# Attention scores as a stream of full banks, a ring of three probability buffers, and a last row tile in column parts

## The chip, the cores and the metric

One Trainium2 chip; the program runs on one of its cores. The metric is the device time of one execution in microseconds (us). TensorE (PE) multiplies matrices and writes its results to PSUM, which the kernel uses as eight banks of 512 fp32 values per partition. ScalarE (ACT), VectorE (DVE) and GpSimd (POOL) work element by element; ACT and DVE read PSUM here. SyncE (SP) issues most of the transfers of the DMA engines, in its program's order; POOL and ACT issue some.

## The reference

Causal attention with 16 "beacon" keys that every query may see, and then a two-layer network with a squared ReLU on the attention's output.

```python
B, H, S, Nb, D = (8, 8, 576, 16, 64)
k_all = np.concatenate([beacon_k, k], axis=2)          # 592 keys per head
v_all = np.concatenate([beacon_v, v], axis=2)
scores = scale * np.matmul(q, k_all.transpose(0, 1, 3, 2))
causal = np.zeros((S, Nb + S), dtype=bool)
causal[:, Nb:] = np.triu(np.ones((S, S), dtype=bool), k=1)
scores = np.where(causal, -1000000000.0, scores)
a = np.exp(scores - scores.max(-1, keepdims=True))
a /= a.sum(-1, keepdims=True) + 1e-09
attn_out = np.matmul(a, v_all)                          # [8, 8, 576, 64]
x = attn_out.transpose(0, 2, 1, 3).reshape(B * S, H * D)  # 4608 tokens x 512
r = np.maximum(x @ w_in, 0.0)                           # w_in 512 x 2048
out = (r * r) @ w_out                                   # w_out 2048 x 512
```

The kernel computes in bf16 with fp32 sums. It leaves the maximum out of the exponential and divides by the sum at the end.

## The kernel before, in words

**Tiling.** Keys and queries are cut into five tiles (`NT`) of 128 positions; the last has 80. The kernel works on pairs of heads: 8 batches of 4 pairs, 32 pairs. Scores are computed transposed, keys on the partitions and queries along the row, so that the exponentials can be the stationary operand of the next matmul. Only what the causal mask leaves is computed: key tile `c` meets the queries from its own start to 576. That makes 1664 columns a pair for each head.

**Scores** (L589). The two heads of a pair sit on partitions 0 to 63 and 64 to 127, and a matmul for each head uses half of PE's rows. They write to a *strip*, two PSUM banks, one per head. There are two strips. In batches 1 to 7 a pair has four pieces of 496, 464, 416 and 288 columns (`WHOLE`), and PE visits the scores twice a pair: two pieces fill both strips, and four more matmuls per head the next two. That is eight visits a batch. Batch 0 has its own cut (`SPLIT`), in two phases, one piece a visit.

**Exponentials** (L604): ACT reads both heads of a piece at once and writes bf16 probabilities to a buffer `pt`; there are four, one for each pair in flight. **Mask** (L614, L618): DVE takes the smaller of the probabilities and 0 or a large number on the diagonal blocks. Four blocks go in one instruction, and the last block of 80 in a second one. **Values** (L639): 15 matmuls for each head with the probabilities as weights and 65 columns of `vb`, v with a column of ones that gives the sum. **Normalise** (L657, L659): DVE divides, into `xn`. Then `xn` is transposed into `xT`: on PE for batches 0 to 2 (L707), by DMA transposes that SP issues for later ones (L690).

**The network.** Chunks of 512 tokens. First layer (L770): 16 tiles of four matmuls, each in a bank, evicted with ReLU by ACT (L786) or DVE (L788), squared by DVE (L795). Second layer (L805): for each of four row tiles of 128 tokens 16 matmuls into one bank, a copy to `osb` (L297 on ACT, L299 on DVE), and a store for every two row tiles (L833), in the last chunk for each (L831).

**PSUM** is full: two strips (four banks) and a pool `ps` of four banks for everything else: first layer, second layer, values, transposes.

**Loads.** q, k and v come in fp32 into eight staging buffers `stg` (L344), are cast by POOL (L299), and for batches 2 to 7 q and k are transposed into `qT` and `kT` by two DMA transposes a batch (L376). SP's queue holds these loads, these transposes, those of `xn` and the stores, in one order. POOL issues the loads of batches 0 and 1 and of the weights.

**The order** is worked out when the program is built. Every piece of work is an `Op` with a duration, a priority, what it needs and which buffers it takes from pools; `Order.run` (L67 on) walks through time, gives each engine the ready piece of least priority value, and so fixes each engine's instruction order. Score pieces also have a gate (L559): they may not start before a certain amount of network work has been placed. On the chip only the order is left, with semaphores for the needs.

## Time and profile before

| | |
|---|---|
| runs | 345.93, 347.67, 347.45 us; median 347.45 |
| the profiled execution: span, first to last instruction | 345.0 us (its own time is given only as this span) |
| PE busy | 327.1 us, 95% |
| ACT busy | 194.7 us, 56% |
| DVE busy | 168.4 us, 49% |
| POOL busy | 90.7 us, 26% |
| score matmuls, L589 | 400, 36.0 us |
| exponentials, L604 | 128, 103.6 us |
| masks, L614 and L618 | 36 and 32; 23.6 and 11.5 us |
| values matmuls, L639 | 960, 40.3 us |
| first and second layer, L770 and L805 | 133.2 and 131.2 us |
| granted PE clock | 1.00 |

Busy time of PE counts each matmul from its start to a modelled end, and matmuls overlap, so a busy PE says that there was no gap and not how fast it was; differences between starts say that. Some matmul records are missing (551 of 576 are there for L805), so a group of three may have been four. In the timeline a line is: start, length, engine, line, operation, tiles, shape, count, and in brackets the idle time before it with what ended it. In the table by stretch a line is: stretch, length, then busy time and count of PE, weight loads, DVE, ACT and POOL, granted clock, DMA share, GB/s.

### The profile page before, as it was taken

The numbers are of one execution on the slowest core, as the hardware profiler recorded it, in microseconds if no ns is written. First come the engines' busy times: TensorE is split into PE (matmuls) and PEld (weight loads), VectorE is DVE, ScalarE is ACT, GpSimd is POOL, SyncE is SP. The second block draws the span as 40 slices with busy tenths as digits, with TensorE's granted clock in tenths as the row PEclk, the third lists the DMA queues.
The fourth block names the chain that finished last, engine by engine and source line by source line (L and its number), as shares of the span: only waits on it lengthen the run. The fifth ranks groups of instructions, "written<-read, shape, count | busy, mean of one in ns | idle before, by whom it ended". The sixth has DMA issues, their size and how long they took to land.

```text
span 345.0 us, 7128 instructions
## 1 busy us (share of the span) xinstructions
PE 327.1 (95%) x2829; PEld 174.0 (50%) x2868; DVE 168.4 (49%) x372; ACT 194.7 (56%) x297; POOL 90.7 (26%) x141
## 2 busy tenths in 40 slices
PE   2799899999998999999999999999999999999995
PEld 1567675544553444444456855544554444444442
DVE  5888884158534873575355546457533302401400
ACT  4796674377645764576656655577536416515611
POOL 9844703316414504250153115312000000000000
PEclk9999999999999999999999999999999999999999
DMA  9999969999999999998699979984014011011002
GB/s 169 220 206 220 205 101 209 214 240 211 177 219 198 232 182 170 209 221 176 142 256 207 178 148 208 228 204 101 2 64 128 0 61 63 0 61 64 0 21 101
DMA packets 145291, 51.88 MB, mean 150 GB/s; under 512 B 132458, under 2 KB 140010, under 8 KB 145258
## 3 DMA queue, kind: packets, MB, share of 16 engines
q1 hardware_dynamic: 135741, 42.45, 61.4%
q0 software_dynamic: 8512, 8.49, 14.5%
q10 hardware_dynamic: 1005, 0.49, 0.6%
q8 instruction: 22, 0.36, 0.5%
q14 instruction: 11, 0.09, 0.1%
HBM read 37.22 MB, written 9.44 MB: 135 GB/s over the span
## 4 chain that ended last, share of the span: by engine, by line
PE 78%; DMA 11%; SPq 3%; ACT 3%; POOL 2%; issue 1%; DVE 1%; DVEq 0%; ACTq 0%; POOLq 0%
PE ps L805 32%; PE ps L770 31%; PE ps L639 7%; DMA stg<-in_v_dram 6%; PE strip L589 6%; ACT pt L604 2%; DMA stg<-in_k_dram 2%; DMA stg<-in_q_dram 1%; DMA osb<-in_k_dram 1%; SPq L344 1%; SPq L376 1%; POOL vb L299 1%; POOL qk_area L299 1%; PE ps L451 1%; PE ps L707 0%
## 5 line engine op out<-in xcount | busy, mean ns | idle before, releaser
L770 PE MATMUL ps<-xT,w_in 128*128 128x512 bf16 (+3 forms) x690 | 133.2, 340 | 0.6
L805 PE MATMUL ps<-w_out,g 128*128 128x512 bf16 x551 | 131.2, 379 | 1.9 <-issue 0.8
L604 ACT ACTIVATE pt<-strip 128x832 bf16<-128x832 f32 (+4 forms) x128 | 103.6, 867 | 38.4 <-PE strip L589 38.2
L786 ACT ACTIVATE g<-ps 128x512 bf16<-128x512 f32 (+2 forms) x128 | 72.0, 562 | 47.9 <-PE ps L770 47.4
L770 PEld LDWEIGHTS <-w_in 128*128 128x128 bf16 x704 | 65.2, 98 | 57.6 <-issue 6.5
L795 DVE TENSOR_TENSOR g<-g 128x1024 bf16<-128x1024 bf16 (+2 forms) x80 | 52.4, 659 | 76.5 <-ACT g L786 75.3
L805 PEld LDWEIGHTS <-g 128*128 128x128 bf16 x576 | 52.5, 98 | 60.0 <-issue 3.2
L299 POOL CAST qk_area<-stg 128x512 bf16<-128x512 f32 (+2 forms) x60 | 39.3, 662 | 53.2 <-DMA stg<-in_k_dram 31.8
L299 POOL CAST vb<-stg 128x512 bf16<-128x512 f32 (+1 forms) x38 | 26.2, 697 | 87.4 <-DMA stg<-in_v_dram 83.0
L297 ACT COPY osb<-ps 128x512 f32<-128x512 f32 x26 | 15.2, 586 | 50.8 <-PE ps L805 44.5
L639 PEld LDWEIGHTS <-pt 128*128 128x128 bf16 (+1 forms) x960 | 36.4, 98 | 14.7 <-issue 3.4
L639 PE MATMUL ps<-vb,pt 128*128 128x65 bf16 (+1 forms) x960 | 40.3, 194 | 3.0 <-POOL vb L299 2.9
L589 PE MATMUL strip<-qT,kT 64*128 64x80 bf16 (+7 forms) x400 | 36.0, 283 | 2.2 <-ACT pt L604 1.0
L659 DVE TENSOR_TENSOR xn<-ps,rcp 128x320 bf16<-128x320 f32 (+2 forms) x64 | 31.5, 492 | 2.4 <-DVE rcp L657 0.2
L614 DVE TENSOR_TENSOR pt<-pt,tri 128x1024 bf16<-128x1024 bf16 (+1 forms) x36 | 23.6, 656 | 13.4 <-ACT pt L604 13.4
L657 DVE RECIPROCAL rcp<-ps 128x5 f32<-128x5 f32 (+2 forms) x64 | 12.3, 192 | 34.6 <-PE ps L639 34.4
L788 DVE TENSOR_SCALAR g<-ps 128x512 bf16<-128x512 f32 (+2 forms) x32 | 19.1, 599 | 9.9 <-PE ps L770 9.2
L589 PEld LDWEIGHTS <-kT 64*128 64x128 bf16 x400 | 12.8, 95 | 21.6 <-issue 17.0
L299 DVE COPY osb<-ps 128x512 f32<-128x512 f32 x10 | 6.9, 692 | 14.9 <-PE ps L805 14.6
L618 DVE TENSOR_TENSOR pt<-pt,tri 80x160 bf16<-80x160 bf16 x32 | 11.5, 359 | 0.0
L344 POOL DMA_DIRECT2D stg<-in_v_dram x10 | 8.5, 854 | 6.9 <-DMA w_in<-in_moe_w_in_dram 5.5
L451 PE MATMUL ps<-ident,qk_area 120*128 120x120 bf16 x16 | 2.5, 299 | 6.5 <-DVE qk_area L299 6.4
(39 smaller groups left out, 68.6 us busy)
## 6 DMA issues: line engine op xcount, KB each, us to landing
out_dram<-osb SPq DMA_DIRECT2D x17, 512.0 KB, 3.7
stg<-in_q_dram SPq DMA_DIRECT2D x24, 256.0 KB, 4.9
stg<-in_k_dram SPq DMA_DIRECT2D x18, 256.0 KB, 5.2
stg<-in_v_dram SPq DMA_DIRECT2D x18, 256.0 KB, 4.7
w_in<-in_moe_w_in_dram POOLq DMA_DIRECT2D x4, 512.0 KB, 11.1
w_out<-in_moe_w_out_dram POOLq DMA_DIRECT2D x4, 512.0 KB, 11.6
stg<-in_v_dram POOLq DMA_DIRECT2D x6, 256.0 KB, 8.4
stg<-in_k_dram SPq DMA_DIRECT2D x6, 224.0 KB, 4.2
```

The lines of the kernel that those rows point to most:

```text
L297: nc.scalar.copy(dst, src)
L299: eng[e].tensor_copy(dst, src)
L589: nc.tensor.matmul(st[:, hj, at:at + t1 - t0], kT[b % 2][hp, pr, 128 * c:128 * c + 128], qT[b % 2][hp, pr, t0:t1], start=True, stop=True,)
L604: nc.scalar.activation(pt[take_pt.held[2]][:, :, off:off + width], st[:, :, 0:width], AF.Exp, bias=0.0, scale=scale)
L614: nc.vector.tensor_tensor(out=d, in0=d, in1=tri[:, m0:m0 + m, :][:, None].to_broadcast([128, 2, m, 128]), op=ALU.min)
L639: nc.tensor.matmul(a[:, at + (t - tl[0]) * (D + 1):at + (t - tl[0] + 1) * (D + 1)], P[0:rr, hj, o:o + 128], vb[b % 2][0:rr, c, 2 * pr + hj ...
L659: nc.vector.tensor_tensor(out=xn[b % 2].rearrange("p t (h d) -> p h t d", d=D)[:, h0:h0 + nh, tl[0]:tl[0] + nt], in0=a[:, :, :, 0:D], in1= ...
L770: nc.tensor.matmul(h[:, lo - spans[0][0]:hi - spans[0][0]], w_in_sb[:, mc, ft * 128:(ft + 1) * 128], xT[:, mc, lo % RING:lo % RING + hi - lo],
L786: nc.scalar.activation(dst, h, AF.Relu, bias=0.0, scale=1.0)
L788: nc.vector.tensor_scalar(out=dst, in0=h, scalar1=0.0, scalar2=None, op0=ALU.max)
L795: nc.vector.tensor_tensor(out=d, in0=d, in1=d, op=ALU.mult)
L805: nc.tensor.matmul(o, G[:, fc, ts * 128:(ts + 1) * 128], w_out_sb[:, fc, :], start=(fc == 0), stop=(fc == NFT - 1))
```

## The change

Three things.

*Scores of batches 1 to 7.* The four pairs of a batch are laid end to end: 4 x 1664 columns are 13 pieces of exactly 512, so that each head's half of a piece fills one bank. The segments of a pair are ordered anew (`SEGS`), and a piece may end one pair and begin the next. A batch has five visits of 2, 3, 3, 3, 2 pieces (2, 2, 3, 3, 3 in batches 1 and 2, `PLAN`). The first two pieces of a visit go to the strips. The third takes two banks of the pool `ps`, one for each head, and its exponentials are one instruction for each head. A piece that wraps around the ring of probabilities has its exponential in two parts.

*Probabilities.* One buffer that holds three pairs of 1664 columns in a ring, instead of four buffers of 2048; batch 0 has a spare slot for its fourth pair. The gaps that had to be cleared are gone, and so are eight memsets. Masks are three instructions a pair (two blocks, two blocks, the last 80), each of which waits only for the exponentials of its own columns. Batch 0's pieces are cut to the same 1664 columns: 368, then 416, 416 and 464. The gate of a visit is computed from where its first column lies. An `Op` may now take from several pools.

*The last row tile.* The last 128 tokens' second layer is done in column parts of 256, 128 and 128, each with its own 16 matmuls, its own copy (DVE, ACT, DVE) and its own store (SP, SP, ACT).

The planner's durations for scores, masks and values are changed a little too, and so the order of everything else shifts.

```diff
-        self.take = (*take, 1)[:3] if take else None
-        self.give = give
+        self.take = [(*t, 1)[:3] for t in (take if isinstance(take, list) else [take])] if take else []
+        self.give = give if isinstance(give, list) else [give] if give is not None else []
...
-    NSTG, NPT, RB = 8, 4, 4
+    NSTG, NPT, RB = 8, 3, 4
+    PW = 1664
...
-    pt = [sb(f"pt{i}", [128, 2, 2048], BF16) for i in range(NPT)]
+    pt = sb("pt", [128, 2, NPT * PW], BF16)
+    pt_spare = sb("pt_spare", [128, 2, PW], BF16)
...
-    for p in pt:
-        nc.vector.memset(p[:, :, 928:1952].rearrange("p h (a w) -> p h a w", w=512)[:, :, :, 0:96], 0.0)
-        nc.vector.memset(p[:, :, 1824:2048], 0.0)
...
+    SEGS = [(0, 0, 240), (0, 368, 576), (1, 112, 576), (2, 240, 576), (3, 368, 576), (4, 496, 576), (0, 240, 368)]
+    seg_at, whole_off = [0], {}
+    for c, t0, t1 in SEGS:
+        for t in range(c, NT):
+            if t0 <= t_start(t) and t_start(t) + t_rows(t) <= t1:
+                whole_off[c, t] = seg_at[-1] + t_start(t) - t0
+        seg_at.append(seg_at[-1] + t1 - t0)
+    assert seg_at[-1] == PW and len(whole_off) == NT * (NT + 1) // 2
...
-        pieces=[
-            ([(0, 0, 496, 0)], 0, 496),
-            ([(1, 112, 576, 0)], 512, 464),
-            ([(2, 240, 576, 0), (0, 496, 576, 336)], 1024, 416),
-            ([(3, 368, 576, 0), (4, 496, 576, 208)], 1536, 288),
-        ],
-        diag=(0, 512, 0, 4), last=1744, tiles=range(NT), off=whole_off)]
+        pieces=None,
+        diag=[(0, 448, 0, 2), (912, 336, 2, 2), (1456, 0, 1, 1)],
+        tiles=range(NT), off=whole_off)]
...
-                ([(2, 240, 576, 0), (4, 496, 576, 336)], 512, 416),
-                ([(3, 368, 576, 0), (0, 240, 496, 208)], 1024, 464),
-                ([(1, 240, 576, 0), (0, 496, 576, 336)], 1536, 416),
+                ([(2, 240, 576, 0), (4, 496, 576, 336)], 368, 416),
+                ([(3, 368, 576, 0), (0, 496, 576, 208), (1, 240, 368, 288)], 784, 416),
+                ([(1, 368, 576, 0), (0, 240, 496, 208)], 1200, 464),
...
+    def slot_of(p):
+        return (p - HP) % NPT if p >= HP else p
+
+    def prob(p):
+        if p < HP and slot_of(p) == NPT:
+            return pt_spare
+        return pt[:, :, slot_of(p) * PW:(slot_of(p) + 1) * PW]
+
+    def freed(p):
+        if p < HP:
+            return []
+        return av_ops[p - NPT] if p >= HP + NPT else av_ops[p - HP]
...
+    PLAN = {1: (2, 2, 3, 3, 3), 2: (2, 2, 3, 3, 3)}
+
+    def add_stream(b):
+        for pr in range(HP):
+            p = HP * b + pr
+            qk_ops[p], av_ops[p], exps_of[p] = [], [], []
+        done, k = 0, 0
+        for n in PLAN.get(b, (2, 3, 3, 3, 2)):
+            visit, pairs, cols = [], [], 0
+            for k in range(k, k + n):
+                mms, outs = [], []
+                lo, hi = 512 * k, 512 * k + 512
+                for pr in range(HP):
+                    for i, (c, t0, t1) in enumerate(SEGS):
+                        a = pr * PW + seg_at[i]
+                        z = a + t1 - t0
+                        if a < hi and z > lo:
+                            x, y = max(a, lo), min(z, hi)
+                            mms.append((pr, c, t0 + x - a, t0 + y - a, x - lo))
+                            cols += max(64, y - x)
+                    x, y = max(pr * PW, lo), min((pr + 1) * PW, hi)
+                    if x < y:
+                        if pr not in pairs:
+                            pairs.append(pr)
+                        outs.append((pr, x, y))
+                visit.append((mms, outs, lo))
+            k += 1
+            first = HP * b + pairs[0]
+            base = 100.0 * first
+            box = {}
+
+            def banks(box, s):
+                qk = box["qk"]
+                if s < 2:
+                    st = strips[qk.slots["strip"][s]]
+                    return st[:, 0], st[:, 1]
+                return tuple(ps[i] for i in qk.slots["ps"])
+
+            def emit_qk(e, visit=visit, box=box):
+                for s, (mms, _, _) in enumerate(visit):
+                    for pr, *mm in mms:
+                        score_mm(b, pr, banks(box, s), *mm)
+
+            deps = []
+            for pr in pairs:
+                deps += qk_deps(b, pr, 0) + freed(HP * b + pr)
+            at = HP * b + visit[0][2] / PW
+            qk = add(f"qk{first}.{k}", "PE", 0.21 + cols / 2400.0, emit_qk, prio=base + k, deps=deps,
+                     take=[("strip", "strip", 2)] + ([("ps", "sc", 2)] if n > 2 else []), gate=gate_at(at))
+            box["qk"] = qk
+            for pr in pairs:
+                qk_ops[HP * b + pr].append(qk)
+            for s, (mms, outs, lo) in enumerate(visit):
+                runs = []
+                for pr, x, y in outs:
+                    p = HP * b + pr
+                    a = slot_of(p) * PW + x - pr * PW
+                    if runs and runs[-1][0] + runs[-1][1] - runs[-1][2] == a:
+                        runs[-1][1] = y
+                        runs[-1][3].append((p, x - pr * PW, y - pr * PW))
+                    else:
+                        runs.append([a, y, x, [(p, x - pr * PW, y - pr * PW)]])
+                for hjs in ([(0, 1)] if s < 2 else [(0,), (1,)]):
+                    prev = []
+                    for i, (a, y, x, whose) in enumerate(runs):
+                        def emit_exp(e, a=a, x=x, y=y, lo=lo, hjs=hjs, box=box, s=s):
+                            if len(hjs) == 2:
+                                out, in_ = pt[:, :, a:a + y - x], strips[box["qk"].slots["strip"][s]][:, :, x - lo:y - lo]
+                            else:
+                                out, in_ = pt[:, hjs[0], a:a + y - x], banks(box, s)[hjs[0]][:, x - lo:y - lo]
+                            nc.scalar.activation(out, in_, AF.Exp, bias=0.0, scale=scale)
+
+                        give = None
+                        if i == len(runs) - 1:
+                            give = (qk, s, "strip") if s < 2 else (qk, hjs[0], "ps")
+                        ex = add(f"exp{first}.{k}.{s}.{hjs[0]}.{i}", "ACT", 0.18 + len(hjs) * (y - x) / 1200.0, emit_exp,
+                                 prio=(base + k + 0.1 * s + 0.01 * hjs[0]) * 1.0e-4 - (30.0 if b > 1 else 12.0), deps=[qk], behind=prev, give=give)
+                        prev = [ex]
+                        for p, r0, r1 in whose:
+                            exps_of[p].append((ex, r0, r1))
+            while done < HP and (done + 1) * PW <= 512 * k:
+                add_phase(b, done, HP * b + done, 0, WHOLE[0])
+                done += 1
...
+        masks = []
+        for i, (at, step, m0, m) in enumerate(ph.diag):
+            rows, w = (128, 128) if step else (LAST, LAST)
+
+            def emit_mask(e, at=at, step=step, m0=m0, m=m, rows=rows, w=w):
+                d = prob(p)[0:rows, :, at:at + max(w, m * step)].rearrange("p h (c w) -> p h c w", c=m)[:, :, :, 0:w]
+                nc.vector.tensor_tensor(out=d, in0=d, in1=tri[0:rows, m0:m0 + m, 0:w][:, None].to_broadcast([rows, 2, m, w]),
+                                        op=ALU.min)
+
+            lo, hi = at, at + (m - 1) * step + w
+            masks.append(add(f"mask{p}.{n}.{i}", "DVE", 0.12 + 2 * m * w / 1920.0, emit_mask, prio=base + 0.1 * i,
+                             deps=[ex for ex, x, y in exps_of[p] if x < hi and y > lo] + [tri_op]))
...
+                     deps=masks + [ex for ex, _, _ in exps_of[p]] + [cast[b, "v", c] for c in range(tl[-1] + 1)]
+                     + av_ops[p][-1:], take=("ps", "av"))
...
+    def add_last(j, ts, base, G, sq):
+        u = 2 * j + ts // 2
+        t0 = j * TCH + ts * 128
+        for n, (c0, c1) in enumerate([(0, 256), (256, 384), (384, 512)]):
+            prev, first = None, {}
+            for hf in range(2):
+                def emit_s2(e, hf=hf, first=first, c0=c0, c1=c1):
+                    o = ps[first["s2"].held[2]]
+                    for fc in range(8 * hf, 8 * hf + 8):
+                        nc.tensor.matmul(o[:, 0:c1 - c0], G[:, fc, ts * 128:(ts + 1) * 128],
+                                         w_out_sb[:, fc, c0:c1], start=(fc == 0), stop=(fc == NFT - 1))
+
+                prev = add(f"s2.{j}.{ts}.{n}.{hf}", "PE", 8 * (c1 - c0 + 6) / 2400.0, emit_s2,
+                           prio=base + 130 + 2 * n + hf, deps=sum(sq[4 * hf:4 * hf + 4], []) + [prev],
+                           take=None if hf else ("ps", "mlp"), pe_time=8 * (c1 - c0 + 6) / 2400.0)
+                first.setdefault("s2", prev)
+
+            def emit_ev(e, first=first, c0=c0, c1=c1):
+                copy_on(e, osb[u % 2][:, ts % 2, c0:c1], ps[first["s2"].held[2]][:, 0:c1 - c0])
+
+            ev = add(f"ev{j}.{ts}.{n}", ("DVE", "ACT", "DVE")[n], 0.2 + (c1 - c0) / 1000.0, emit_ev, prio=-15.0,
+                     deps=[prev] + st_ops[u - 2], give=first["s2"])
+
+            def emit_st(e, c0=c0, c1=c1):
+                {"SP": nc.sync, "ACT": nc.scalar}[e].dma_start(
+                    out=out[t0:t0 + 128, c0:c1], in_=osb[u % 2][:, ts % 2, c0:c1])
+
+            add(f"st{j}.{ts}.{n}", ("SP", "SP", "ACT")[n], 0.65, emit_st, prio=-20.0, deps=[ev], dma=0.3)
...
+            if j == NCH - 1 and ts == TCH // 128 - 1:
+                add_last(j, ts, base, G, sq)
+                continue
...
-        for pr in range(HP):
-            add_pair(b, pr)
+        if b < NSPLIT:
+            for pr in range(HP):
+                add_split_pair(b, pr)
+        else:
+            add_stream(b)
```

## The prediction

> **What bounds the kernel now.** I read four views, in this order: the slices, the stretches, the waits, and the timeline where a wait stood.
>
> The slices first: TensorE (PE) is busy nearly everywhere, and the DMA engines are too for the first two thirds.
>
> ```profile
> PE   2799899999998999999999999999999999999995
> DMA  9999969999999999998699979984014011011002
> ```
>
> Then busy time by stretch. The clock is 1.00 throughout, so no time is lost to it:
>
> ```profile
> 25.00:72.60 47.60, 46.19 (x522) 29.67 (x524) 29.44 (x70) 26.95 (x48) 17.95 (x27) 1.00 1.09 189
> 72.60:109.40 36.80, 34.60 (x322) 17.52 (x327) 19.75 (x41) 23.92 (x33) 14.09 (x20) 1.00 1.12 213
> 109.40:241.00 131.60, 130.20 (x1169) 69.20 (x1188) 76.41 (x154) 82.13 (x117) 39.13 (x60) 1.00 0.99 192
> 241.00:341.20 100.20, 99.61 (x570) 46.81 (x579) 24.75 (x46) 43.27 (x70) 0.37 (x1) 1.00 0.13 43
> ```
>
> After 109 us PE is dense, and from 241 us DMA (0.13) no longer matters. Before 109 us DMA is full (1.09 and 1.12) and PE has holes. The waits and the timeline say which:
>
> ```profile
> PE ps L639 <- POOL vb L299: 2.9, 4, 1.2
> PE strip L589 <- ACT pt L604: 1.0, 4, 0.4
> ```
>
> (line waited for: us in total, times, longest), from the page on the score matmuls' line the time that their weight loads sat idle,
>
> ```profile
>   DMA kT<-qk_area: 0.4, 1
> ```
>
> and from the timeline of PE (start, length):
>
> ```profile
> 72.67 0.58 PE L589 MATMUL strip<-qT,kT 64*128 64x496 bf16 x4
> ...
> 108.35 0.31 PE L639 MATMUL ps<-vb,pt 128*128 128x65 bf16 x5 [0.57 <-POOL vb L299]
> 109.44 0.19 PE L639 MATMUL ps<-vb,pt 80*128 80x65 bf16 x1 [0.78 <-POOL vb L299]
> ```
>
> So the first scores of batch 2 start at 72.67 the moment kT lands, and the first probabilities-times-V of batch 3 wait for the last cast of v until 109.4. Anything that merely makes PE faster ahead of those two points waits there. Last, what a visit to the scores costs:
>
> ```profile
> 203.20 0.58 PE L589 MATMUL strip<-qT,kT 64*128 64x496 bf16 x4
> 203.71 2.76 PE L805 MATMUL ps<-w_out,g 128*128 128x512 bf16 x12
> 206.41 0.48 PE L589 MATMUL strip<-qT,kT 64*128 64x336 bf16 x8
> 206.82 1.04 PE L805 MATMUL ps<-w_out,g 128*128 128x512 bf16 x4
> 207.69 0.62 PE L639 MATMUL ps<-vb,pt 128*128 128x65 bf16 x15
> ```
>
> Read the differences of starts. Dense matmuls of 512 columns take 0.2157 us each (0.86 us per four). The twelve from 203.71 take 2.70, 0.11 more than 2.59. The two heads run side by side, so 496+464 columns should take 0.40; the visit takes 0.51. The one of 336+80+208+80 columns should take 0.30 and takes 0.41. A visit thus costs about 0.10 on the way in and 0.11 inside, **0.21 us**, whether it has two or four segments per head. Entering from the values matmuls costs the same.
>
> **The change, part by part.**
>
> *Fewer visits.* In the built order, runs of score matmuls fall from 69 to 47: 22 x 0.21 = 4.62 us less PE work. The columns are the same (4 x 1664 = 13 x 512 per batch). Score matmuls go from 400 to 618. A segment of 80 columns cost no more than its columns, as the visit of 0.41 shows. Those of 16, 16, 32 and 48 columns have no row; I floor them at 64 columns, near the 65 of the values matmuls (15 in 0.46, 31 ns each with its weight load): 0.06 us a batch, 0.4 in all. Bounds: nothing, or 31 ns for every one of the 218 added, 6.8 us; the 80-column row is nearest, so 0.4. Pricing every matmul of both orders like this gives 324.7 us before and 320.5 after. Before, 324.7 plus 12.0 of start (first values of batch 1 at 39.44, 27.4 of work ahead) plus the waits gives 341, where PE does end (341.2).
>
> *What of it lies ahead of a DMA.* I counted the work ahead of each point in both orders, and when its data was ready before:
> - kT of batch 2, ready 72.6: work 59.05 before, 57.40 after. The changed PE arrives near 57.4+12.5 = 69.9 and waits 2.7. Work left: 265.6 and 263.1.
> - v of batch 3, ready 109.4: work 93.66 and 90.35; left 231.0 and 230.2.
> - v of batch 4, cast by 134.5, not waited for before: 121.63 and 122.10. In the new SP order the five xT transposes of batch 3 (6.4 us on the queue from 131.72) stand ahead of the last three v loads, so ready near 140.9; left 198.4.
> - v of batch 7, ready 241.4: 225.15 and 223.40; left 99.5 and 97.1.
>
> If those times stand, PE ends no earlier than 72.6+263.1 = 335.7, 109.4+230.2 = 339.6, 140.9+198.4 = 339.3, 241.4+97.1 = 338.5. Three of four agree on about 339. One thing pulls them in: on SP, a store of 512 KB that stood after the second v load of batch 3 (issued 99.01, 0.53 us) now comes five issues later, and one in batch 2 two loads later. That frees 0.5 us of queue at least and 2.5 us of DMA (512 KB at the 213 GB/s of the stretch) at most ahead of the 109.4. I take 1 us there, nothing for batch 4 beyond 0.5, and 339.0.
>
> *The start.* Batch 0's pieces are cut anew and its values end 17.58 us into PE's work, not 15.75. On POOL the last cast of v for batch 1 comes before two zeroings (1.0 us) instead of after, which takes most of the 1.2 us wait at 41.27 away. Both lie ahead of the kT wait, which covers up to 2.7 us of loss and swallows any gain, so 0.
>
> *Waits inside the visits.* A visit of three pieces needs both strips and two of the four ps banks at once; its exponentials are two of 1024 (992 took 0.996) and two of 512 (near 0.60), 3.2 us on ACT. Queued behind are relu and evictions on ACT, and behind them PE's next bank. Cover is DVE (49% busy) and the second-layer matmuls, which hold one bank for 3.45 us. Most such visits in the order have 8 to 20 of these next to them. The row for such waits is 1.0 us in all before; I take 0.2 more, bounds 0 and (below, the slower rival) 7.
>
> *Probability ring of three pairs.* Scores of a pair now wait for the values of three pairs earlier rather than four. These stand earlier on PE itself, so no wait of its own; both bounds are the 0 of PE's own order and the 0.4 longest wait seen on ACT.
>
> *ACT and DVE.* Exponentials for batches 1 to 7 go from 112 to 121: 9 x 0.2 = 1.8 us on ACT at 56%. Masks go from one of 1024 (0.724) to two of 512 (0.415): 28 x 0.11 = 3 us on DVE. The AV of a pair now waits per segment. Covered while ACT and DVE idle over 40%; uncovered at most 5 us.
>
> *Clearing of pt gone.* Eight memsets, 1.9 us on DVE from 1.49 to 3.29; the first cast waits for DMA until 3.62, so 0.
>
> *Last rows in column parts.* Before, the last matmul ends at 341.2:
>
> ```profile
> 341.03 1.23 SPq L831 DMA_DIRECT2D out_dram<-osb  x2
> 341.29 0.59 ACT L297 COPY osb<-ps 128x512 f32<-128x512 f32 x1 [0.29 <-PE ps L805]
> ```
>
> Copy 0.59, store landing 2.0 after its issue, about 1.1 to the end: 3.8. After, a DVE copy of 128 columns (512 take 0.692 and 272 take 0.437, so near 0.28), then the same store from ACT. I give the smaller store no shorter landing (bounds: 0 to 1 us gained). 0.3 gained. Cost on PE: 32 matmuls of 128 columns where 8 of 512 stood, priced by columns at 54 ns. The values row (31 ns with a weight load) puts them between 31 and 108 ns (the 256-column ones).
>
> The Trainium skill speaks against this: "TensorE: Matmul & The Clock Gate", Back-to-back issue gap, puts a stream of weight load and matmul at about 81 ns for 128 columns. By it the tail would lose 32 x 27 ns = 0.9 us and the parts would cost 0.6 net instead of gaining 0.3. That page's own 131 ns for 512 columns does not agree with the 216 measured here, so I go by the rows. The skill's "DMA: Bandwidth & Descriptors", Anatomy of one DMA, gives some 2.0 us fixed per transfer; by that a quarter of the bytes gains little, as the 2.0 of the 256 KB row already has it.
>
> **Sum.** PE ends at 339.0 + 0.2 = 339.2, tail 3.5: span 342.7 against 345.0, 2.3 less. The page gives the execution's own time only as its span; the three runs are 345.93 to 347.67, median 347.45, 2.45 above it. Carried over: **345.1 us**.
>
> **The rivals.**
> 1. *All of it hidden by DMA.* v of batch 4 or 7 comes another 1 to 2 us later, because the transposes now in front of the loads also wait for the norms. Speaks for it: DMA at 0.99 to 241 us. Against: the same bytes. PE ends at 340.2 to 341.5, 346.0 to 347.5 with the tail.
> 2. *No DMA wait counts* after 72.6: the moved stores bring v3 and v4 in by 3 us. 335.7+3.5 is 339.2: 341.6 to 343.
> 3. *Slower: banks.* Two of four ps banks lie behind 3.2 us of exponentials, where first-layer matmuls (0.86 a bank) follow. PE fills the other two in 1.7 and stands for up to 1.5. There are 21 visits with three pieces, some 7 beside first-layer work. Against it: DVE can take a bank in 0.69. If all lose on average 0.21 (4.5/21), nothing is left of the gain; at 0.35 it is 7.4 us lost and 4.5 gained, 350.3. It decides from 0.3 per visit.
> 4. *The cost is per bank or piece and not per visit*, so merging removes nothing: then 0.06 a batch and the masks remain, 347.5. Against: two segments or four, the same 0.21.
>
> **How the numbers follow.** 0.5% is 1.7 us, about what a measurement here can tell from no change. Forecast (343.2 to 345.7) 0.48; rival 2 0.13; rival 1 and 4 together 0.23; rival 3 0.16. Faster 0.61, same 0.22, slower 0.17. For 8 in 10 I go from rival 2's lower end to past the unchanged time into the weaker form of rival 3: 341.5 to 348.8.
>
> **What the changed profile would show.** Right: about 47 score runs; dense advance of 0.4 per 960 columns plus 0.21 a visit; PE's wait on kT near 72.6 grown to 2 us or more; a wait on vb near 108 and perhaps near 140; last copy 128 columns of about 0.28. Wrong: waits of PE's ps matmuls on ACT pt (rival 3); no wait on vb (rival 2); a visit of five segments costing 0.5 more than its columns (rival 4).

## The result and the profile after

The changed kernel took **344.7 us** (median of 12 runs, 342.99 to 346.62), the kernel before 346.2 beside it (12 runs, 344.87 to 347.67). The ratio is **0.9952, 95% interval 0.9929 to 0.9975**: 1.5 us faster, 0.8 to 2.5. The profiled execution has a span of 341.3 us and took 342.99, so it is the fastest of the twelve: read against the 345.0 of before, it shows a gain of 3.7 us, more than the median run has. (A run takes about 1.7 us more than its span, so the 345.0 of before stands for a run of some 346.7, half a microsecond above its median.)

The slices of the profile after look like those of before:

```profile
PE   2899989999999999999999999999999999999996
DMA  9999979999999997997799889989024011011003
```

Busy time by stretch, with the limits used before (stretch, length, busy time and count of PE, weight loads, DVE, ACT, POOL, granted clock, DMA share, GB/s):

```profile
25.00:72.60 47.60, 45.54 (x562) 30.25 (x561) 28.74 (x71) 29.16 (x53) 17.51 (x27) 1.00 1.10 197
72.60:109.40 36.80, 35.24 (x389) 20.01 (x394) 24.42 (x55) 23.96 (x36) 15.26 (x22) 1.00 1.12 213
109.40:241.00 131.60, 130.23 (x1296) 74.52 (x1314) 74.69 (x166) 82.12 (x122) 37.32 (x59) 1.00 0.96 189
241.00:338.30 97.30, 96.59 (x584) 47.48 (x591) 24.59 (x47) 41.94 (x70) 0.00 (x0) 1.00 0.14 46
```

The hole before 109 us has moved: PE was busy for 46.19 and 34.60 us in the first two stretches, now for 45.54 and 35.24. What PE waits for (line waited for: us in total, times, longest) says what kind of hole it is now:

```profile
PE ps L889 <- DVE qT L296: 0.7, 1, 0.7
PE ps L729 <- DVE g L907: 0.7, 2, 0.3
...
PE ps L797 <- DVE xn L749: 0.6, 2, 0.4
...
PE ps L729 <- DVE xn L749: 0.3, 1, 0.3
PE ps L927 <- DVE osb L296: 0.3, 1, 0.3
PE ps L889 <- DVE osb L296: 0.3, 1, 0.3
...
PE ps L889 <- DVE xT L296: 0.2, 1, 0.2
```

The 2.9 us of waits for `vb` are gone. In their place stand waits for DVE that were not there before, all of matmul groups that write to the pool `ps` (L889 and L927 first and second layer, L729 values, L797 transposes). By the timeline, nine tenths of this, eight waits of 2.8 us together, lie between 39 and 109 us; one of L797's two comes at 18 us. The first of the eight comes ahead of the first visit of three pieces, and the other seven, 2.1 us, behind it:

```profile
39.17 2.14 PE L889 MATMUL ps<-xT,w_in 128*128 128x272 bf16 x16 [0.67 <-DVE qT L296]
...
41.69 0.63 PE L578 MATMUL strip<-qT,kT 64*128 64x64 bf16 x10
42.16 0.39 PE L578 MATMUL ps<-qT,kT 64*128 64x48 bf16 x10
```

PE's timeline at the points that the prediction named, and at some visits:

```profile
71.70 0.61 PE L578 MATMUL strip<-qT,kT 64*128 64x240 bf16 x10
...
105.55 0.62 PE L729 MATMUL ps<-vb,pt 128*128 128x65 bf16 x15
...
227.16 0.61 PE L578 MATMUL strip<-qT,kT 64*128 64x240 bf16 x10
227.71 2.76 PE L889 MATMUL ps<-xT,w_in 128*128 128x512 bf16 x11
230.40 0.62 PE L578 MATMUL strip<-qT,kT 64*128 64x224 bf16 x12
230.85 0.38 PE L578 MATMUL ps<-qT,kT 64*128 64x64 bf16 x4
231.17 3.77 PE L889 MATMUL ps<-xT,w_in 128*128 128x512 bf16 x16
```

The first scores of batch 2 (71.70) and the values of batch 3 (105.55) start without idle time: kT had landed at 70.96 (before: 72.28), and the last cast of v for batch 3, which starts being used within that group, ended at 105.85. Two-piece visits take 0.55 from start to start for 1024 columns (0.43 by columns), three-piece visits 0.77 for 1536 (0.64).

The end of the timeline, all engines:

```profile
336.77 1.50 PE L844 MATMUL ps<-w_out,g 128*128 128x128 bf16 x24
...
338.38 0.29 DVE L296 COPY osb<-ps 128x128 f32<-128x128 f32 x1 [3.16 <-PE ps L844]
338.70 0.38 ACTq L859 DMA_DIRECT2D out_dram<-osb  x1
```

The last copy takes 0.29 instead of 0.59. From the last matmul's end (338.28) to the end of the span (341.25) it is 2.97 us, before 3.79.

### The profile page after: what moved, and what is told of

Same layout as the page of the kernel before. It is cut to its first block, busy times and chain, and to the rows that moved or that the text cites. A ratio compares the mean times of both kernels' runs of the same rounds, so it can differ in the third digit from the quotient of the medians.

```text
span 341.3 us, 7642 instructions
## 1 busy us (share of the span) xinstructions
PE 324.8 (95%) x3077; PEld 184.4 (54%) x3118; DVE 168.9 (49%) x392; ACT 194.3 (57%) x308; POOL 89.3 (26%) x141
## 4 chain that ended last, share of the span: by engine, by line
PE 88%; DVE 4%; DMA 3%; ACT 2%; issue 1%; SPq 1%; POOL 0%; POOLq 0%; DVEq 0%
PE ps L889 35%; PE ps L927 34%; PE ps L729 8%; PE strip L578 6%; DMA stg<-in_v_dram 1%; PE ps L578 1%; DMA osb<-in_k_dram 1%; PE ps L844 1%; PE ps L797 1%; ACT pt L607 1%; PE ps L450 1%; DVE kT L296 1%; SPq L340 1%; DVE xn L749 1%; DVE qT L296 0%
## 5 line engine op out<-in xcount | busy, mean ns | idle before, releaser
L889 PE MATMUL ps<-xT,w_in 128*128 128x512 bf16 (+3 forms) x690 | 132.3, 340 | 2.0 <-DVE qT L296 0.7
L927 PE MATMUL ps<-w_out,g 128*128 128x512 bf16 x533 | 127.3, 379 | 2.1 <-issue 0.6
L889 PEld LDWEIGHTS <-w_in 128*128 128x128 bf16 x704 | 66.3, 98 | 55.5 <-issue 4.0
L685 ACT ACTIVATE pt<-strip 128x1024 bf16<-128x1024 f32 (+3 forms) x75 | 68.5, 967 | 27.6 <-PE strip L578 27.6
L927 PEld LDWEIGHTS <-g 128*128 128x128 bf16 x560 | 51.4, 98 | 57.9 <-issue 3.4
L294 ACT COPY osb<-ps 128x512 f32<-128x512 f32 (+1 forms) x24 | 13.6, 572 | 60.0 <-PE ps L927 60.0
L707 DVE TENSOR_TENSOR pt<-pt,tri 128x512 bf16<-128x512 bf16 (+1 forms) x93 | 36.7, 412 | 19.4 <-ACT pt L685 18.1
L729 PEld LDWEIGHTS <-pt 128*128 128x128 bf16 x930 | 35.2, 98 | 11.8 <-issue 2.1
L729 PE MATMUL ps<-vb,pt 128*128 128x65 bf16 x930 | 38.0, 194 | 1.2 <-DVE g L907 0.7
L578 PE MATMUL strip<-qT,kT 64*128 64x128 bf16 (+13 forms) x496 | 28.4, 244 | 1.2 <-DVE kT L296 0.5
L578 PEld LDWEIGHTS <-kT 64*128 64x128 bf16 x618 | 20.3, 95 | 14.8 <-issue 10.9
L685 ACT ACTIVATE pt<-ps 128x512 bf16<-128x512 f32 (+3 forms) x46 | 23.4, 584 | 0.0
L296 DVE COPY osb<-ps 128x512 f32<-128x512 f32 (+2 forms) x14 | 9.0, 644 | 25.1 <-PE ps L927 12.4
L607 ACT ACTIVATE pt<-strip 128x832 bf16<-128x832 f32 (+2 forms) x12 | 10.0, 879 | 0.3 <-PE strip L578 0.2
```

Source lines behind the costliest of these rows:

```text
L294: nc.scalar.copy(dst, src)
L296: eng[e].tensor_copy(dst, src)
L578: nc.tensor.matmul(st[hj][:, at:at + t1 - t0], kT[b % 2][hp, pr, 128 * c:128 * c + 128], qT[b % 2][hp, pr, t0:t1], start=True, stop=True,)
L685: nc.scalar.activation(out, in_, AF.Exp, bias=0.0, scale=scale)
L707: nc.vector.tensor_tensor(out=d, in0=d, in1=tri[0:rows, m0:m0 + m, 0:w][:, None].to_broadcast([rows, 2, m, w]), op=ALU.min)
L729: nc.tensor.matmul(a[:, at + (t - tl[0]) * (D + 1):at + (t - tl[0] + 1) * (D + 1)], P[0:rr, hj, o:o + 128], vb[b % 2][0:rr, c, 2 * pr + hj ...
```

## Experiments

Two theories on what became of the PE work that was saved (4.15 us by the prediction's prices):

- **A, the data.** PE still arrives at k, q and v about as they land, so what it saves ahead of a landing is lost there. This is what the prediction had.
- **B, the banks.** A third piece of a visit takes two of the four `ps` banks, and the groups that share the other two wait until DVE has emptied them.

Beside them the tail is tested, the smaller ring, and DVE's load. "Ratio" is always to the kernel before, run beside it (its medians were 346.1, 345.7 and 346.0 us in the three sets); in brackets the 95% interval.

### The tail, from both sides, and the changed kernel again

The changed kernel once more, for comparison on the same chip:

> The changed kernel once more, to see a second of its executions. In the first profile its span is 341.3 us, and its twelve timed runs lie between 342.99 and 346.62 us, 1.7 us above their spans. Theory A (DMA): the runs differ by waits of PE on kT and on vb, which that profile does not have (before: 2.9 us on vb). A slower execution then shows 1 to 3 us of them, and PE's other waits stay as they are. Theory B (banks): what the change loses is PE's waits for ps banks and for DVE between 39 and 109 us, near 3 us (0.67 on qT, 0.65 on L907, 0.6 on osb, 1.0 on xn). They are there in every execution alike, and no wait on vb. Ratio to before 0.993 to 0.998 by both.

Measured: 344.22 us, ratio 0.9943 [0.9920, 0.9966]. The profile of this run (342.1 us) has the eight waits for DVE between 39 and 109 us again, 2.4 us together, as theory B had it, and 0.7 us for v of batch 7, less than the 1 to 3 us that theory A asked for in a slow one (line waited for: us in total, times, longest):

```profile
PE ps L729 <- POOL vb L296: 0.7, 2, 0.4
```

The changed kernel without the column parts:

```diff
-            if j == NCH - 1 and ts == TCH // 128 - 1:
-                add_last(j, ts, base, G, sq)
-                continue
```

> The changed kernel with the last row tile done whole, as before: one bank, one copy of 512 columns, one store. The profiles have 3.8 us from the last matmul's end to the end before and 3.0 after. If the column parts are worth that, this kernel is 0.5 to 0.9 us slower than the changed one, its tail is 3.6 to 3.9, and its ratio to before is near 0.997. My forecast had 0.3: 0.996. If the page's 81 ns a matmul held, it would be no slower or 0.6 faster.

Measured: 345.79 us, ratio 0.9987 [0.9963, 1.0012]; 4.0 us from the last matmul to the end.

The kernel before with the column parts alone (the function `add_last` and those three lines):

> The kernel before with the last row tile in column parts and nothing else. If they are worth 0.75 us by themselves: ratio 0.998, PE's end as before (341.2) and a tail of 3.0. If my 0.3: 0.999. If 81 ns a matmul of 128 columns: PE's end 0.9 later, ratio 1.000 to 1.002.

Measured: 345.76 us, ratio 0.9986 [0.9964, 1.0009]; 2.98 us from the last matmul to the end.

The parts are worth 0.0044 of 346 us, 1.5 us, where they are taken out, and 0.0014, 0.5 us, where they are put in. The intervals hold both with the 0.8 to 1.0 us that the ends of the traces differ by. That is over half of what the whole change is worth, and more than the 0.3 forecast. The copy took 0.3 less. The stores, by the view of transfers (size, median us from issue to landing), have most of the rest:

```profile
out_dram<-osb SPq DMA_DIRECT2D x1, 256.0 KB, 2.1
...
out_dram<-osb SPq DMA_DIRECT2D x1, 64.0 KB, 1.9
...
out_dram<-osb ACTq DMA_DIRECT2D x1, 64.0 KB, 1.6
```

The last store, 64 KB issued by ACT, landed about 0.4 us sooner than a whole one issued by SP (2.0 before). How much of this is its size and how much its queue isn't shown: the other store of 64 KB, issued by SP, took 1.9.

### No score piece in the pool of banks

The changed kernel with visits of two pieces at most, seven a batch instead of five:

```diff
-        for n in PLAN.get(b, (2, 3, 3, 3, 2)):
+        for n in (2, 2, 2, 2, 2, 2, 1):
...
-                     take=[("strip", "strip", 2)] + ([("ps", "sc", 2)] if n > 2 else []), gate=gate_at(at))
+                     take=[("strip", "strip", min(n, 2))] + ([("ps", "sc", 2)] if n > 2 else []), gate=gate_at(at))
```

> The changed kernel with seven visits a batch of two pieces each (2,2,2,2,2,2,1), all in the strips: no score piece in the ps banks. Theory: a visit costs 0.21 us, so the 14 more give 2.9 us more PE work than the changed kernel. Theory B (banks): the waits of PE on DVE and on ps banks between 39 and 109 us (near 3 us) go, and the kernel is within 0.5 us of the changed one. Theory A (DMA): those waits do not matter or stay, and the time rises by 1.5 to 2.9 us, ratio to before 1.000 to 1.004. If the cost is per piece and not per visit, the time stays as in the changed kernel and PE's dense work too.

Measured: **343.31 us** (342.72 to 343.92), ratio **0.9910 [0.9886, 0.9934]**. It has 61 score visits instead of 47 and 2.9 us more PE work, and it is 0.9 us below the changed kernel beside it (the intervals overlap by a little). Of PE's waits after 35 us these are the longest:

```profile
PE ps L729 <- POOL vb L296: 0.9, 2, 0.7
...
PE ps L889 <- DVE qT L296: 0.6, 1, 0.6
```

All waits for DVE but one are gone, and waits for v are back. Banks and data both show, so the next runs take the data's lateness down. (With another plan of visits the planner also orders the other work anew, here and in every run below that changes the visits; so it takes several plans, and the place of the waits, to tell the banks from the order.)

### The same with lighter transfers

In the kernels from here on the 37 transposing DMA transfers are plain copies of as many bytes: the transposition is left out, so the output is that of other numbers, and the rest of the work is the same.

```diff
             nc.sync.dma_start(
-                out=dst[b % 2].rearrange("p g (c t) -> p (g c) t", c=NT),
-                in_=srcb[b % 2].rearrange("p g c d -> p (g c d)"),
-                transpose=True,
-            )
+                out=dst[b % 2], in_=srcb[b % 2].rearrange("p g c d -> p g (c d)"))
...
-                nc.sync.dma_start(out=xT[:, :, at:at + n], in_=xn[b % 2][0:n, t, :], transpose=True)
+                nc.sync.dma_start(out=xT[:, :, at:at + n],
+                                  in_=xn[b % 2][:, t, :].rearrange("p (m c) -> p m c", c=128)[:, :, 0:n])
```

The kernel before with plain copies:

> The kernel before, with each of its 37 transposing transfers (12 for q and k, 25 for xn) replaced by a plain copy of as many bytes between the same tiles: the transposition is left out, everything else is computed. The trace of before charges its hardware queue, which carries the transposes, with 61 per cent of the time of the 16 DMA engines, and PE with 2.9 us of waits for v. Expected by every theory: the waits for loaded data get shorter, ratio 0.985 to 0.995 against the kernel before (the 2.9 us of waits and up to 2 more); it is the base for the other kernels with plain copies. If the ratio is within 0.002 of 1, the transposes weren't what made the data late.

Measured: 345.14 us, ratio 0.9974 [0.9957, 0.9990], less than the 0.985 to 0.995 expected. The transposes were a small part of the lateness: 1.7 us of waits for v are left in the profile.

The changed kernel with plain copies:

> The changed kernel with the same plain copies in place of the transposes (transposition left out). Theory A (the data): what the changed kernel saves on PE was swallowed because PE arrives at k, q and v almost as they land; with lighter transfers it shows in full, 4.15 us of PE work and 0.8 of tail, so 4.5 to 5 us below the kernel before with plain copies. Theory B (the banks): the three-piece visits take two of the four ps banks, and PE waits about 3 us more for VectorE to empty the others, loaded data or not; so only 1.5 to 2.5 us below it.

Measured: 344.09 us, ratio 0.9941 [0.9919, 0.9963], the same as with the transposes (0.9943 and 0.9952), and only about 1.1 us below the kernel before with plain copies. PE waits for no v and no kT of a later batch any more, and the waits for DVE behind the three-piece visits are where they were, among them:

```profile
PE ps L725 <- DVE g L904: 0.7, 2, 0.3
...
PE ps L725 <- DVE xn L745: 0.3, 1, 0.3
PE ps L924 <- DVE osb L296: 0.3, 1, 0.3
PE ps L886 <- DVE osb L296: 0.3, 1, 0.3
```

Theory A, which asked for 4.5 to 5, falls; B's 1.5 to 2.5 was a little too much.

Two pieces at most, with plain copies:

> The changed kernel with visits of two pieces at most, in seven visits per batch instead of five, none of whose pieces lies in ps banks, and with plain copies in place of the transposes (transposition left out). Its PE work is 2.9 us more than that of the changed kernel. Theory A (the data): with the data early, work counts, so it is 2 to 3 us slower than the changed kernel with plain copies. Theory B (the banks): its waits for VectorE are gone with the data early too, so it is 0.5 to 1.5 us faster than the changed kernel with plain copies, as it was with the transposes (343.3 against 344.2).

Measured: 341.97 us, ratio 0.9906 [0.9883, 0.9929]. With early data too, 2.9 us more work is about 1.2 us faster than the changed kernel (0.0035 of 346), as B had it.

Two pieces in batches 1 and 2 alone:

```diff
-    PLAN = {1: (2, 2, 3, 3, 3), 2: (2, 2, 3, 3, 3)}
+    PLAN = {1: (2, 2, 2, 2, 2, 2, 1), 2: (2, 2, 2, 2, 2, 2, 1)}
...
-                     take=[("strip", "strip", 2)] + ([("ps", "sc", 2)] if n > 2 else []), gate=gate_at(at))
+                     take=[("strip", "strip", min(n, 2))] + ([("ps", "sc", 2)] if n > 2 else []), gate=gate_at(at))
```

> Visits of two pieces in batches 1 and 2 alone, where the trace of the changed kernel shows the waits of PE for VectorE (39 to 86 us), and of up to three pieces from batch 3 on; with plain copies in place of the transposes (transposition left out). Its PE work is 321.4 us by my prices, 0.9 more than the changed kernel's and 2.1 less than that of two pieces everywhere. Theory B (the banks, early ones): the fastest of the kernels with plain copies, 1 to 2 us below two pieces everywhere. Theory B with the waits spread over all batches: between the two others. Theory A (the data): 0.5 to 1 us slower than the changed kernel with plain copies.

Measured: **340.70 us, ratio 0.9864 [0.9838, 0.9891]**, the fastest of all, though with the transposition left out. (The intervals of this kernel and of two pieces everywhere, 0.9906, overlap by a little.) The 15 three-piece visits of batches 3 to 7 do what they were made for.

The reverse, three pieces in batches 1 and 2 and two from batch 3 on:

> The complement of the kernel with two pieces in batches 1 and 2: visits of up to three pieces in batches 1 and 2, of two pieces at most from batch 3 on, plain copies in place of the transposes (transposition left out). PE work 322.6 us by my prices, 2.1 more than that of the changed kernel with plain copies. Theory B with early banks alone: the waits stay and the work comes on top, 1.5 to 2.5 us slower than the changed kernel with plain copies, 345.6 to 346.6 us. Theory B with the waits spread over the batches: as fast as it or up to 1 us faster, since no score piece takes a ps bank in five batches out of seven.

Measured: 345.06 us, ratio 0.9979 [0.9959, 0.9998]: about 1.3 us slower than the changed kernel with plain copies (0.0038; 1.5 to 2.5 expected) and 4.0 slower than its complement, of which 1.2 is PE work by the prices (322.6 against 321.4). The loss sits in batches 1 and 2.

Two pieces in batch 1 alone (the entry for batch 2 left as it was):

> Visits of two pieces at most in batch 1 alone, of up to three from batch 2 on, plain copies in place of the transposes (transposition left out). PE work 320.9 us by my prices. In the trace of the changed kernel with plain copies PE falls back for VectorE by about 1.7 us between 43 and 60 us (batch 1) and by another 1.3 between 80 and 110 us (batches 2 and 3). If each batch's waits come from its own three-piece visits: 1 to 1.5 us faster than the changed kernel with plain copies, and 1 to 1.5 slower than two pieces in batches 1 and 2. If the first batch starts the delay and the later waits only follow from it: as fast as the latter.

Measured: 341.48 us, ratio 0.9871 [0.9843, 0.9900], no different from two pieces in batches 1 and 2. One wait of 0.3 us for DVE is left in batch 2, though its visits have three pieces again; the second of the two expectations is right. Why batch 2 no longer loses isn't settled: the planner also ordered the work differently from there on.

### Where PE falls back

A table of lags makes this plain. The lag of an instruction on PE is its start less the PE work ahead of it in its order, priced as the prediction did (0.21 a visit, columns at 2.4 per ns, 0.2157 per 512); I worked it out from every kernel's trace, at three amounts of work (about 40, 110 and 335 us into the span).

```
                                        lag at 28   at 95   at 318 us of work
before                                    13.19     15.40     16.15
changed                                   12.01     15.87     17.36
changed, again                            11.80     15.66     18.25
changed, two pieces                       12.27     13.33     14.78
with plain copies:
  changed                                 11.02     14.98     16.34
  three pieces in batches 1 and 2 only    11.28     14.84     15.57
  two pieces in batch 1                   12.72     13.72     15.22
  two pieces in batches 1 and 2           11.25     11.92     13.61
  two pieces                              12.39     12.64     13.34
  ring of four                            12.75     16.20     17.24
  less squaring on VectorE                13.13     16.94     18.30
```

Wherever batch 1 has three-piece visits PE falls back by 3.4 to 4.0 us between the first two columns; without them by 0.25 to 1.1. Before, it was 2.2, of which the wait for v of batch 3 is some 1.5. In the changed kernel nearly all of it stands at the seven waits for DVE: by differences of starts they cost 0.3 to 0.65 us each, 3.6 in all. The brackets of the timeline show 2.1, because they count from a modelled end of the matmuls. From there on, with plain copies, kernels with three-piece visits lose 1.0 to 1.7 and those with two-piece ones 0.7, so 0.02 to 0.07 us for each of 15 visits. That holds whatever happened in the first 40 us, where executions differ by 2 us. (The profile of the kernel before with plain copies lost clock, 0.94 between 20 and 45 us, and is left out.)

The table also closes the account of the two profiles first compared. Work, 324.7 to 320.5: -4.15. Lag at 28, where the wait of 1.2 us for v of batch 1 went: -1.2. From 28 to 95, 3.86 against 2.21: +1.65, which is the waits for the banks less those for v of batch 3. From 95 to the end, 1.49 against 0.75: +0.7. Tail: -0.8. Together -3.8, where the spans differ by 3.7.

### What the banks wait for

DVE made faster in that stretch, by squaring only 64 columns in the first two chunks (the rest is left unsquared); the order of all instructions is that of the changed kernel:

```diff
-                    d = G[:, 2 * f:2 * f + 2, lo:hi]
+                    d = G[:, 2 * f:2 * f + 2, lo:lo + 64 if j < 2 else hi]
```

> The changed kernel with plain copies (transposition left out), and the squaring on VectorE in the first two chunks done on 64 columns only instead of the chunk's 512 (or 240 and 272): the other columns are left unsquared. The order of all instructions and PE's work are the same. It takes about 7 us out of 40 that VectorE is busy between 40 and 110 us. If PE waits because VectorE comes late to the banks: 1 to 2 us faster than the changed kernel with plain copies, with fewer and shorter waits of PE for VectorE. If it waits because the planner put two matmul groups on one bank so close together that any VectorE would be late: less than 0.5 us faster.

Measured: 343.67 us, ratio 0.9941 [0.9920, 0.9963], the changed kernel's with plain copies, although DVE was busy for 35.4 us instead of 40.1 between 40 and 110 us. By the table PE fell back by 3.81 us there, against 3.96. (That is 4.7 us less; 7 were expected.) So a DVE with about an eighth less to do doesn't shorten these waits; as far as this test goes, its load is not what makes them. The timeline of the changed kernel (with transposes) around one of them, all engines:

```profile
47.29 0.38 PE L578 MATMUL ps<-qT,kT 64*128 64x176 bf16 x8
...
47.60 0.63 PE L729 MATMUL ps<-vb,pt 128*128 128x65 bf16 x15
...
48.07 0.63 PE L889 MATMUL ps<-xT,w_in 128*128 128x272 bf16 x4
48.27 0.20 DVE L747 RECIPROCAL rcp<-ps 128x5 f32<-128x5 f32 x1 [0.53 <-PE ps L729]
...
48.50 0.49 DVE L749 TENSOR_TENSOR xn<-ps,rcp 128x320 bf16<-128x320 f32 x1
48.73 0.40 ACT L905 ACTIVATE g<-ps 128x272 bf16<-128x272 f32 x1 [0.39 <-PE ps L889]
...
49.03 1.02 ACT L685 ACTIVATE pt<-strip 128x1024 bf16<-128x1024 f32 x1
49.04 0.62 PE L729 MATMUL ps<-vb,pt 128*128 128x65 bf16 x15 [0.35 <-DVE xn L749]
...
49.93 1.22 ACT L685 ACTIVATE pt<-ps 128x384 bf16<-128x384 f32 x4
```

The third score piece is written to its two banks at 47.29, and ACT empties them only from 49.93 to 51.15, after the visit's two strips. Meanwhile the two other banks take one values group (47.60) and one first-layer group (48.07). DVE stands idle for 0.53 us until the values are there, then needs 0.72 us (48.27 to 48.99) for reciprocal and product, and PE's next group starts right after it, at 49.04. By columns the first-layer group was through at 48.53, so the wait costs PE 0.51 us. Next in PE's order is another values group, which needs a bank, and with two of four held by scores there is none until then. With the lighter DVE the same wait, at the same place in PE's order, is as long:

```profile
50.11 0.62 PE L725 MATMUL ps<-vb,pt 128*128 128x65 bf16 x15 [0.35 <-DVE xn L745]
```

In later batches few groups of that short kind lie next to a visit: at 231.17 above, sixteen matmuls of the first layer follow it, four groups of 0.86 us with one emptying each. That this is why the later visits lose so little is argued from the orders and not tested by itself.

### The ring

Four pairs in the ring instead of three (the spare buffer, then unused, shrinks to make room):

```diff
-    NSTG, NPT, RB = 8, 3, 4
+    NSTG, NPT, RB = 8, 4, 4
...
-    pt_spare = sb("pt_spare", [128, 2, PW], BF16)
+    pt_spare = sb("pt_spare", [128, 2, 8], BF16)
```

> The changed kernel with plain copies (transposition left out) and a ring of four pairs of probabilities instead of three, as many as the kernel before had. PE work is the same, the order of the instructions moves a little. If the smaller ring costs nothing, as my sum had it: within 0.5 us of the changed kernel with plain copies. If it makes the scores wait for the values of the pair three before: 1 to 2 us faster.

Measured: 343.63 us, ratio 0.9936 [0.9914, 0.9959]; with three pairs 0.9941. The smaller ring costs nothing that shows.

Not measured: two pieces in batches 1 and 2 with the transposes left in. Among the kernels with all the work, two pieces everywhere is the best that ran, faster than both kernels compared here.

## Why the prediction was right, and where it was wrong

The time, 345.1 forecast and 344.7 measured, was right, as a difference too: 2.3 us forecast from a median of three runs, 1.5 measured, with the interval reaching to 2.5. Two of its terms were wrong in opposite directions: it counted on a loss at the DMAs that didn't come, and put the loss at the banks, which did, at 0.2. It also carried 2.45 us over from span to time; a run here has some 1.7 between its own span and its time, and the rest was how far one profiled execution lay from a median.

- **Fewer visits** (4.62 less 0.4): the mechanism was right. A visit of three pieces costs 0.13 above its columns from its start to the next group, one of two 0.12, so the price is per visit, and rival 4 falls. With 10 visits more in batches 3 to 7 and 2.1 us more work by its prices, two pieces everywhere lost 0.0042, 1.45 us, against two pieces early. The 0.65 between is 0.04 for each of the 15 three-piece visits, within what they lose by the table of lags, so it needs no other price.
- **What of it lies ahead of a DMA** is the step that failed. It had PE wait 2.7 us for kT of batch 2 and again for v of batches 3, 4 and 7. None of these waits is in the profile. The reading of kT was off to begin with: before, kT had landed at 72.28, and PE came to it at 72.67 by its own work (68.25, twenty matmuls of 0.2157 and the 0.10 of the way in), so it didn't wait there. Now kT landed at 70.96. The last cast of v for batch 3 was done by 105.85 instead of 109.39, 3.5 us earlier where 1 was allowed, and v of batch 4 was cast by 137.72, not 140.9. The first load of v for batch 3 was issued 1.6 us sooner already (95.70, before 97.27), and no store stands among these loads any more; what each of the two gave isn't shown. PE arrived at kT at 71.70 and not at 69.9, because it had already lost time at the banks. It now arrives within a microsecond of the data at all four points, which is why a wait for v of 0.7 us shows in the second profile of the same kernel. But lighter transfers gained the changed kernel nothing. Rival 2's sign, no wait on v, came; its time, 341.6 to 343, didn't.
- **Waits inside the visits** (0.2, bounds 0 to 7): mis-sized. PE falls back by 3.4 to 4.0 us from batch 1 to batch 3, against 0.25 to 1.1 where batch 1 has visits of two pieces. The bounds held it; the value taken from the row nearest, which was a kernel with four free banks, did not.
- **Rival 3** named the banks and the first-layer work beside them, and "decides from 0.3 per visit": over 21 visits it came to about 0.18. It expected PE to wait for ACT's exponentials. PE waits for the turn of the other two banks through DVE, and only early.
- **Last rows in column parts** (0.3): 0.8 to 1.0. The copy was right (0.28 forecast, 0.29 measured); the smaller store was given no shorter landing and landed 0.4 us sooner. The Trainium skill's "DMA: Bandwidth & Descriptors", Anatomy of one DMA, has about 2.0 us fixed for a transfer, in a section on transfers that GpSimd issues. These stores are issued by SP and ACT: 256 KB took 2.0 to 2.1, 128 KB 1.7, 64 KB 1.9 by SP and 1.6 by ACT, so less than 2.0 is fixed here. The cost on PE that "TensorE: Matmul & The Clock Gate", Back-to-back issue gap, would have added (81 ns a matmul of 128 columns) did not come: the chain of work has the last 24 in 1.35 us, 56 ns each.
- **Start** (0): the wait of 1.2 us for v of batch 1 went, as said. It was to be swallowed by the wait for kT; that did not come, so the 1.2 counts.
- **Ring, ACT, DVE** (0): the ring and DVE's load were tested above, and neither shows a cost. The clearing of `pt` and ACT's 1.8 us were not tested by themselves; PE has no wait for ACT after 18 us.

So the forecast lost 3.3 us to the DMAs (PE's end at 339.0 instead of the 335.7 of its first point), the chip fell back by 3.4 to 4.0 at the banks, and the nearness of the two is chance.

## What to carry to other kernels

Before a piece of work is given more buffers of a shared pool, count what the other users of the pool need to keep PE going: not only the emptying engine's load, which gave nothing here, but how many short groups follow each other, and the time from a group's last matmul to its bank's release (the first of these two is argued here from the orders). Where it differs by phase, make the choice by phase; here the same larger visit lost some 0.5 us each in the first two batches, and lost less than it saved in the others. And where PE arrives just as data lands, don't put a missing gain down to the data before a run with earlier data has shown it.

## What the runs showed of the chip that was not expected

PE runs at a lower speed early on, in some executions for 5 us longer than in others, and the granted clock of the views doesn't show it. The first 24 values matmuls in a row, in the timelines of the changed kernel with plain copies and of the one with the lighter DVE, whose PE orders are the same:

```profile
19.53 0.90 PE L725 MATMUL ps<-vb,pt 128*128 128x65 bf16 x24
```

```profile
20.26 1.52 PE L725 MATMUL ps<-vb,pt 128*128 128x65 bf16 x24
```

The views give a granted clock of 1.00 in both. For these microseconds that isn't a measurement: the trace's own record of the clock begins with a grant of the full clock, at 17.11 us in the first and at 22.02 in the second, and the views count time without a record as full. Ahead of the grant the values matmuls start 54 to 55 ns apart, behind it 29. Once both run at full speed the second execution is 1.5 us further behind, as much as the whole change is worth, and at the end 2.0. Four of the eight profiles with plain copies show the later change; in the two profiles first compared the grant stands at 15.04 (before) and 17.73 us (changed). The Trainium skill's "TensorE: Matmul & The Clock Gate", Part 1, says that the warm-up goes by a free-running window, so that its end varies from run to run. It varies here too, but by 4.9 us between two executions with one PE order, where the page has a window of 3.4 us, and no run here shows what decides it.
